# Soft mixture of experts behind a windowed attention: the order of the last unit, the selection of v, and two weight matrices in pieces

## The chip, the cores and the metric

One core of a Trainium2 chip runs the whole program. The metric is the device time of one execution in microseconds; the runs shown for the kernel before are three (184.94, 185.99 and 186.16 us, median 185.99). The profile is of one execution of its own.

The engines of the core are PE (matrix products, with its weight loads shown apart as PEld), DVE (elementwise work and reductions), ACT (activations and copies), POOL (here only an issuer of loads) and SP (issuer of stores). Sixteen DMA engines move data between main memory and the on-chip memory. PE writes to PSUM only.

## The reference

Eight batches, eight heads, 576 positions, 64 wide. Heads 0 to 3 attend to the last 32 positions, heads 4 to 7 to the last 128 positions in steps of 4 (the dilated heads). The outputs of the heads side by side are x, 4608 rows of 512. Then a soft mixture of experts:

```python
scores = np.where(masks, (1 / np.sqrt(D)) * q @ k.T, -1e9)       # per batch and head
x = softmax(scores) @ v                                          # 4608 x 512
logits = x @ phi                                                 # 32 slots, 4 for each of 8 experts
d = exp(logits - logits.max(0)); d /= d.sum(0)                   # over all tokens
slot_input = d.T @ x
for e in range(8): slot_out[e] = np.maximum(slot_input[e] @ w1[e], 0) @ w2[e]
c = exp(logits - logits.max(1)); c /= c.sum(1)                   # over the slots
return c @ slot_out
```

w1[e] is 512 x 1024, w2[e] is 1024 x 512. The slot inputs need the logits of every token, so no expert can start before the attention of the last batch is done, and no output before the last expert is.

## The kernel before

**Units.** The attention is cut into 32 units of two heads (NU = 4 per batch, in the order 0, 2, 1, 3 of `unit`, so that plain and dilated pairs alternate). A unit goes through `transposes` (q and k, L261), `scores` (L300), `softmax_parts` (Exp on ACT, then a product with the mask on DVE, L325), `values` (L367), a reciprocal and a product on DVE that make rows of x (L399, L400), and `x_transposes` (L409), which writes xT. The loop of L611 runs these for different units in one round, so that the engines overlap. In rounds of four, batch by batch, come `front_logits` (L432), `front_rows` (L462) and `front_slots` (L482), which add a batch to the slot inputs in `U_sb`. The last batch is done apart in `last_early`, `last_logits` and `last_slots` (L503 to L549), and ends in `siT` (L654), the slot inputs, transposed.

**Dilated keys and the last 64 positions.** A dilated head is worked on in four classes of positions (position mod 4), 144 positions to a class. 128 of a class make a full block (`P1`). The last 16 of each class stand in `P2` (L360), a block of 32 columns for each head, class and side (one side for keys among the first 128 of the class, one for the last 16), and `values` multiplies each with 32 columns of the array (L390 to L393).

**v.** The plain heads need v by blocks of 128 positions, and the load gives four positions to a partition. `select_v` (L198), once per batch, makes the blocks on PE: products of the raw v with `pick`, a 0/1 matrix, 32 partitions at a time at four places of the array. The last 64 positions come from a load of 16 partitions (`vt`). The results go through PSUM tiles `sel` (two from the pool ps_s, one from `ring`) and are copied by ACT to `vp` (L213, L234). `spread_v` copies the dilated v.

**PSUM.** ps_s has two buffers of two banks for the scores (and `sel`, and `last` in the end), ps_o two for the outputs of `values`, `ring` two for everything else: transposes, logits, rows, slots.

**Order.** A planner sets the order of PE, DVE and ACT from the order of the program, its costs and the free buffers. POOL's order is as written (L599).

**Loads.** POOL issues them all, with a cast from fp32 to fp16. Eight tiles `home` take the raw q, k and v of the eight batches (L154), all issued at the start. When batch e has been read out of its home, `load_w1(e)` and `load_w2(e)` (L236, L245) put the weights of expert e into it: 128 partitions, 1 MB of fp16 each, one transfer, w2[7] in two halves by columns. The order at the end is w1[6], w1[7], w2[6], w2[7]. Eight semaphores are used by turns for POOL's loads.

**Experts.** For each pair of experts `expert_in` (L670) makes the hidden values (64 matmuls L675 in all), ACT applies Relu (`hs`, L683), four transposes (L686) and two copies on DVE (`hTp`, L691) turn them, and `expert_out` (L696) adds to `sop` (L699, 8 matmuls per expert). The order is in(0), in(1), out(0), out(1), in(2), and so on. Then `so` is copied (L716), and for each of 36 blocks of 128 tokens a matmul (L735) and a scaling on ACT or DVE (L739, L741) make the output, stored by SP in 12 transfers (L745, L747).

## Time and profile before

| what | us |
|---|---|
| three runs: lowest, median, highest | 184.94, 185.99, 186.16 |
| profiled execution, from the first to the last instruction (span) | 183.5 |
| median of the runs less the span | 2.4 |
| PE busy, share of the span | 151.8, 83% |
| DVE | 117.1, 64% |
| ACT | 115.5, 63% |
| POOL | 46.9, 26% |
| last rows of x of the attention (L400) end at | 136.2 |
| first matmul of the experts (L675) starts at | 145.0 |
| last half of w2[7] has landed at | 156.74 |
| `so` copied at | 157.8 |
| first store issued at | 158.9 |

The page gives no own time for the profiled execution beside its span; what lies around the span is the start before the first instruction and the end after the last, and the table shows it only as the difference to the median of other runs. A row of the profile names the line, the engine, the operation and the tiles, then how often, how long in all, and in brackets how long the engine had been idle and what ended that. "L205 PE MATMUL sel<-home,pick" is a matmul of line 205 that writes a tile `sel` from `home` and `pick`; a group of rows close in time is merged, and its time then runs from the first start to the last end. A matmul's time includes its way through the array, so matmuls in a row overlap. PEclk is the granted clock of PE. The strips have 40 slices of the span.

### The profile page before, as it was taken

Reading aid. Unit: us, or ns where it says so; the run is one execution under the profiler, and the core shown is the slowest. Engines: PE = TensorE matmul, PEld = TensorE weight load, DVE = VectorE, ACT = ScalarE, POOL = GpSimd, SP = SyncE. Lnnn points to the kernel's source line nnn. Section 1 sums busy time; section 2 is a strip of 40 time slices with the busy share of each in tenths; the row PEclk is TensorE's granted clock in tenths of the full one; section 3 lists DMA queues with packets and bytes.
Section 4 is the critical chain, followed back from the end, with each engine's and each line's share of the span. In section 5 each row is a group of like instructions: output and inputs, shape, how many; then the busy total and the mean of one; then the engine's idle time right before and its main releaser. Section 6 shows DMA issues by size and latency. Waiting matters only on the chain.

```text
span 183.5 us, 6054 instructions
## 1 busy us (share of the span) xinstructions
PE 151.8 (83%) x2595; PEld 105.8 (58%) x2595; DVE 117.1 (64%) x363; ACT 115.5 (63%) x208; POOL 46.9 (26%) x77
## 2 busy tenths in 40 slices
PE   1869999999988989998997998898979998885300
PEld 1637776677676667666765767666768644432000
DVE  7605886388877877878779687786970111496410
ACT  2248845689599789779878959977703022675410
POOL 7752555464554654401102001003100000000000
PEclk9999999999999999999999999999995589998555
DMA  5999999999999999999999999999999995199996
GB/s 103 183 203 203 202 203 201 202 202 204 204 201 201 204 199 204 226 211 221 212 216 216 212 216 216 218 212 218 218 214 220 212 208 105 75 440 427 427 427 262
DMA packets 23978, 41.06 MB, mean 224 GB/s; under 512 B 1680, under 2 KB 20240, under 8 KB 21136
## 3 DMA queue, kind: packets, MB, share of 16 engines
q0 software_dynamic: 21584, 30.79, 93.9%
q1 hardware_dynamic: 2368, 9.89, 13.4%
q8 instruction: 20, 0.33, 0.6%
q14 instruction: 6, 0.05, 0.1%
HBM read 62.02 MB, written 9.44 MB: 389 GB/s over the span
## 4 chain that ended last, share of the span: by engine, by line
DMA 74%; issue 15%; POOL 3%; ACT 2%; DVE 1%; PE 0%; POOLq 0%; DVEq 0%; SPq 0%
DMA home<-in_moe_w_dram 31%; DMA home<-in_v_dram 15%; DMA home<-in_k_dram 12%; DMA home<-in_q_dram 9%; DMA out_dram<-ot 7%; ACT ot L739 2%; DVE ot L741 1%; POOL home L250 1%; POOL home L162 1%; POOL home L239 1%; POOL home L184 0%; POOL home L187 0%; ACT so L716 0%; PE sop L699 0%; PE f L735 0%
## 5 line engine op out<-in xcount | busy, mean ns | idle before, releaser
L400 DVE TENSOR_TENSOR x<-o,rc 128x384 f16<-128x384 f32 x64 | 29.9, 482 | 0.5
L332 ACT ACTIVATE pr<-s 128x960 f16<-128x960 f32 (+1 forms) x32 | 24.7, 780 | 1.8 <-PE s L315 1.8
L344 ACT ACTIVATE pd<-s 128x640 f16<-128x640 f32 x32 | 20.9, 706 | 1.7 <-PE s L315 1.7
L162 POOL DMA_DIRECT2D home<-in_v_dram x24 | 16.6, 692 | 16.6 <-DMA home<-in_k_dram 11.6
L205 PE MATMUL sel<-home,pick 32*128 32x256 f16 x128 | 17.8, 307 | 1.4 <-DMA home<-in_v_dram 1.1
L399 DVE RECIPROCAL rc<-o 128x6 f32<-128x6 f32 x64 | 10.2, 177 | 13.5 <-PE o L395 13.4
L416 PE MATMUL rgx<-ident,x 128*128 128x128 f16 x160 | 15.6, 233 | 3.0 <-ACT qT L295 3.0
L741 DVE TENSOR_SCALAR ot<-f,rrow 128x512 f32<-128x512 f32 (+1 forms) x19 | 12.5, 716 | 7.7 <-DMA out_dram<-ot 5.2
L335 DVE TENSOR_TENSOR Pp<-pr,mask 128x960 f16<-128x960 f16 (+2 forms) x48 | 16.4, 394 | 0.4 <-ACT pr L332 0.4
L280 ACT COPY qT<-rgq 128x576 f16<-128x576 f16 x16 | 10.3, 641 | 9.0 <-PE rgq L275 8.5
L422 ACT COPY xT<-rgx 128x512 f16<-128x512 f16 x16 | 9.6, 601 | 10.0 <-PE rgx L416 10.0
L739 ACT ACTIVATE ot<-f,rrow 128x512 f32<-128x512 f32 (+1 forms) x19 | 11.2, 675 | 7.0 <-DMA out_dram<-ot 6.6
L239 POOL DMA_DIRECT2D home<-in_moe_w_dram x8 | 4.3, 534 | 44.4 <-PE rgq L290 36.5
L213 ACT CAST vp<-sel 128x512 f16<-128x512 f32 x16 | 9.4, 590 | 9.2 <-PE sel L205 9.0
L416 PEld LDWEIGHTS <-x 128*128 128x128 f16 x160 | 10.2, 102 | 7.2 <-issue 5.4
L735 PE MATMUL f<-so,ET 128*128 128x512 f16 (+1 forms) x38 | 11.0, 402 | 3.9 <-ACT ot L739 3.0
L275 PEld LDWEIGHTS <-home 96*64 96x64 f16 x384 | 11.9, 123 | 3.9 <-issue 2.0
L184 POOL DMA_DIRECT2D home<-in_k_dram x16 | 10.6, 661 | 10.1 <-DMA home<-in_q_dram 8.2
L395 PE MATMUL o<-vp,Pp 128*128 128x65 f16 x288 | 12.9, 203 | 0.0
L436 PE MATMUL l<-xT,phi 128*128 128x288 f16 x64 | 10.8, 304 | 2.0 <-ACT qT L280 1.7
L295 DVE COPY kTd<-rgk 128x576 f16<-128x576 f16 x16 | 12.0, 752 | 0.6 <-PE rgk L290 0.5
L295 ACT COPY qT<-rgq 128x576 f16<-128x576 f16 x16 | 10.3, 646 | 3.1 <-PE rgq L290 2.6
(105 smaller groups left out, 292.9 us busy)
## 6 DMA issues: line engine op xcount, KB each, us to landing
home<-in_moe_w_dram POOLq DMA_DIRECT2D x15, 1024.0 KB, 30.1
out_dram<-ot SPq DMA_DIRECT2D x7, 1024.0 KB, 7.5
home<-in_k_dram POOLq DMA_DIRECT2D x16, 288.0 KB, 9.9
home<-in_q_dram POOLq DMA_DIRECT2D x15, 288.0 KB, 9.7
home<-in_v_dram POOLq DMA_DIRECT2D x16, 256.0 KB, 9.8
out_dram<-ot SPq DMA_DIRECT2D x3, 512.0 KB, 6.5
home<-in_moe_w_dram POOLq DMA_DIRECT2D x2, 512.0 KB, 27.3
home<-in_v_dram POOLq DMA_DIRECT2D x8, 64.0 KB, 8.9
```

The lines of the kernel that those rows point to most:

```text
L162: nc.gpsimd.dma_start(out=dst, in_=v[b, h0 : h0 + n_h, r0 : r0 + 4 * n_p, :].rearrange("h (p r) d -> p h (r d)", r=4),)
L205: nc.tensor.matmul(sel[:, n, 0], pick[rows, r].rearrange("p i j -> p (i j)"), raw[rows, :, r, :], start=(r == 0), stop=(r == 3), tile_posi ...
L275: nc.tensor.transpose(rg[64 * h : 64 * h + 64, r, :], raw[:, 2 * hp + h, D * r : D * r + D], ident[0:NP, 0:NP],)
L295: (nc.scalar.copy if nm == "q" else nc.vector.tensor_copy)(out=dst[:, 0:S].rearrange("c (g p a) -> c g p a", g=4, a=3), in_=rg.rearrange(" ...
L332: nc.scalar.activation(out=pr, in_=st[:, :, 0:n], func=AF.Exp, scale=SCALE)
L335: nc.vector.tensor_tensor(out=Pp[:, :, b0 : b0 + nb, 0:w], in0=pr[:, :, at : at + nb * w].rearrange("p h (t c) -> p h t c", c=w), in1=mask ...
L344: nc.scalar.activation(out=pr[:, part].rearrange("p c e t -> p e c t"), in_=st[:, :, 0 : 2 * DW].rearrange("p e (c t) -> p e c t", c=2), f ...
L395: nc.tensor.matmul(to, lhs, rhs, start=(n == 0), stop=(n == len(mms) - 1), skip_group_check=True)
L400: nc.vector.tensor_tensor(out=x[:, blocks[0] : blocks[0] + nb, D * hl : D * hl + 2 * D].rearrange("p t (h d) -> p t h d", h=2), in0=ot[:, ...
L416: nc.tensor.transpose(rg[:, 128 * blk : 128 * blk + 128], x[:, blk, hl : hl + 128], ident)
L739: nc.scalar.activation(out=ot[:, j, d0:d1], in_=fp, func=AF.Copy, scale=scale)
L741: nc.vector.tensor_scalar(out=ot[:, j, d0:d1], in0=fp, scalar1=scale, scalar2=None, op0=ALU.mult)
```

## The change

- **Selection of v.** `pick` has 128 partitions and 132 columns with one 1 in each row, so that a shifted window of 128 columns selects the wanted positions of all partitions: 16 matmuls of 128 rows in place of 16 of 32 rows. The end is 4 matmuls of 16 rows over all eight heads in place of 4 and 4. All three results are tiles of `ring`.
- **The last 16 of each class.** `P2` becomes `Pm` (keys among the first 128) and `Pt` (keys among the last 16), both as blocks of 128 columns with zeros between, made by two DVE products. `values` has five full matmuls per head for them in place of eight narrow ones. The rows of a class end are now in position order, so `x_transposes` copies them plainly, and the logits by rows have 9 blocks in place of 13.
- **Written order.** From the last unit on, PE, DVE and ACT run in the order of the program up to the end of the experts. The loop ends one round earlier, and what is left is written out. `fill` issues matmuls whose result nobody reads: two, one and two of 512 columns. The last logits by tokens go to ps_o. In the experts, `expert_in` of the next pair stands ahead of the transposes (`expert_turn`) and of `expert_out` of this pair.
- **Two w2.** w2[3] and w2[5] are loaded as 112 partitions, and then the last 16 partitions as four transfers of 8: one column block of eight, seven column blocks, one, seven.
- The constants change accordingly: `spread_masks` is gone, `spread_ends` is new, and the transposed phi is made by 16 matmuls in place of 4.

```diff
 RP, NP = 6, 96
 RD, ND = 12, 48
 CL = S // DIL
+TAIL = 16
 DW = CL + 16
 OUT_TILES = [(0, 2), (256, 2)] + [(512 + 512 * i, 4) for i in range(7)] + [(4096, 2), (4352, 2)]
 OUT_COLS = [sum(nj for _, nj in OUT_TILES[:i]) for i in range(len(OUT_TILES))]
 NU = 4 * B
 NV = 2
+UNEVEN = (3, 5)
 
...
-    pick = kept([128, 4, 32, 4], "pick")
+    pick = kept([128, 4, 132], "pick")
+    pick_end = kept([128, 4 * 144], "pick_end")
...
     def select_v(b):
         raw, last = raws[b]["vp"], raws[b]["vt"]
         for i in range(2):
-            sel = ps_s.tile([128, 2, 2, 4, D], FP32, name=f"sel{b}_{i}", tag="s")
-            for r in range(4):
-                for n in range(2):
-                    rows = slice(64 * i + 32 * n, 64 * i + 32 * n + 32)
+            sel = ring.tile([128, 2, 4, D], FP32, name=f"sel{b}_{i}", tag="ring")
+            for n in range(2):
+                for r in range(4):
                     nc.tensor.matmul(
-                        sel[:, n, 0],
-                        pick[rows, r].rearrange("p i j -> p (i j)"),
-                        raw[rows, :, r, :],
+                        sel[:, n],
+                        pick[:, 2 * i + n, 3 - r : 131 - r],
+                        raw[:, :, r, :],
                         start=(r == 0),
                         stop=(r == 3),
-                        tile_position=(64 * i + 32 * n, 0),
                     )
-            nc.scalar.copy(out=vp[b % NV][:, 2 * i : 2 * i + 2, :, 0:D], in_=sel[:, :, 0])
-        end = ring.tile([128, 2, 4, D], FP32, name=f"sel{b}_2", tag="ring")
+            nc.scalar.copy(out=vp[b % NV][:, 2 * i : 2 * i + 2, :, 0:D], in_=sel)
+        end = ring.tile([128, 2, 4, D], FP32, name=f"end{b}", tag="ring")
         for r in range(4):
             nc.tensor.matmul(
-                end[:, 0],
-                pick[96:112, r].rearrange("p i j -> p (i j)"),
-                last[:, 0:4, r, :],
+                end.rearrange("p a h d -> p (a h) d"),
+                pick_end[96:112, 128 * r : 128 * r + 128],
+                last[:, :, r, :],
                 start=(r == 0),
                 stop=(r == 3),
                 tile_position=(96, 0),
-            )
-        for r in range(4):
-            nc.tensor.matmul(
-                end[32 * r : 32 * r + 32, 1],
-                ident[96:112, 96:128],
-                last[:, 4:8, r, :],
-                start=True,
-                stop=True,
-                tile_position=(96, 32 * r),
-                skip_group_check=True,
             )
         nc.scalar.copy(out=vp[b % NV][:, 4:6, :, 0:D], in_=end)
...
     def load_w2(e):
         w2t = w_tiles[e][1]
         w2_from = moe_w2[e].rearrange("(p c) f -> p c f", p=128)
-        parts = ((0, 8),) if e < E_EXP - 1 else ((0, 4), (4, 8))
-        for c0, c1 in parts:
+        parts = [(0, 128, 0, 8)] if e < E_EXP - 1 else [(0, 128, 0, 4), (0, 128, 4, 8)]
+        if e in UNEVEN:
+            parts = [(0, 112, 0, 8)]
+            for p0 in (112, 120):
+                parts += [(p0, p0 + 8, 0, 1), (p0, p0 + 8, 1, 8)]
+        for p0, p1, c0, c1 in parts:
             nc.gpsimd.dma_start(
-                out=w2t[:, c0:c1].rearrange("p c f -> p (c f)"),
-                in_=w2_from[:, c0:c1].rearrange("p c f -> p (c f)"),
+                out=w2t[p0:p1, c0:c1].rearrange("p c f -> p (c f)"),
+                in_=w2_from[p0:p1, c0:c1].rearrange("p c f -> p (c f)"),
             )
 
...
+        tails = pr[:, :, :, 128:DW].rearrange("p a c (s t) -> p a c s t", s=2)
         nc.vector.tensor_tensor(
-            out=P2.rearrange("p a c s t -> p (a c) s t")[:, :, :, 0:16],
-            in0=pr[:, :, :, 128:DW].rearrange("p a c (s t) -> p (a c) s t", s=2),
-            in1=mask[:, QW + 64 :].rearrange("p (c s t) -> p c s t", c=8, s=2),
+            out=Pm.rearrange("p a (c x) -> p (a c) x", c=4)[:, :, 0 : 4 * TAIL : 4],
+            in0=tails[:, :, :, 0].rearrange("p a c t -> p (a c) t"),
+            in1=mask[:, None, 128:CL].broadcast_to([128, 8, TAIL]),
+            op=ALU.mult,
+        )
+        nc.vector.tensor_tensor(
+            out=Pt[:, :, 0 : 4 * TAIL].rearrange("p a (t c) -> p a c t", c=4),
+            in0=tails[:, :, :, 1],
+            in1=ends[:, None].broadcast_to([128, 2, 4, TAIL]),
             op=ALU.mult,
         )
...
                         mms.append((ot[:, i, h], P1[:, h, blk, :], vd[b % 2][:, 4 * (hl + h) + blk, :]))
                     else:
-                        for s in range(2):
-                            for c in range(4):
-                                vt = vp[b % NV][:, 5, hl + h] if s else vd[b % 2][:, 4 * (hl + h) + c]
-                                mms.append((ot[32 * c : 32 * c + 32, i, h], P2[:, h, c, s], vt))
+                        for c in range(4):
+                            mms.append((ot[:, i, h], Pm[:, h, 128 * c : 128 * c + 128], vd[b % 2][:, 4 * (hl + h) + c]))
+                        mms.append((ot[:, i, h], Pt[:, h], vp[b % NV][:, 5, hl + h]))
             for n, (to, lhs, rhs) in enumerate(mms):
                 nc.tensor.matmul(
...
+    def logits(b, c, lp, kcs):
+        for kc in kcs:
+            nc.tensor.matmul(
...
+    def token_weights(b, c, lp):
+        nc.scalar.activation(
+            out=ET[:, b * S + 288 * c : b * S + 288 * c + 288],
...
-    row_blocks = [(slice(0, 128), 128 * i, 1) for i in range(4)]
-    row_blocks += [(slice(0, 128), c, 4) for c in range(4)] + [(slice(0, 128), 512, 1)]
-    row_blocks += [(slice(32 * c, 32 * c + 32), 512 + c, 4) for c in range(4)]
+            logits(b, c, lp, range(4))
+            token_weights(b, c, lp)
+
+    row_blocks = [(128 * i, 1) for i in range(4)] + [(c, 4) for c in range(4)] + [(512, 1)]
 
     def rows(to, tokens, rhs, start, stop):
-        for n, (part, at, step) in enumerate(row_blocks):
-            w = step * (part.stop - part.start - 1) + 1
+        for n, (at, step) in enumerate(row_blocks):
             nc.tensor.matmul(
-                to[part, min(n, 9), :], tokens(at, at + w, step), rhs, start=start, stop=stop,
+                to[:, n, :], tokens(at, at + 127 * step + 1, step), rhs, start=start, stop=stop,
                 skip_group_check=True,
...
-    def last_early(last):
+    def last_open(last):
+        lr = last[:, 1, 0 : 10 * N_SLOTS].rearrange("p (i s) -> p i s", s=N_SLOTS)
+        nc.tensor.matmul(lr[:, 8], ident, shut, start=True, stop=False, skip_group_check=True)
+        return lr
+
+    def last_sums(last, lr):
         six = small.tile([128, 1], FP32, name="six")
         nc.vector.reduce_sum(six, csum, axis=AX.X)
         sixes = small.tile([128, N_SLOTS], FP32, name="sixes")
         nc.vector.tensor_scalar(out=sixes, in0=stackI, scalar1=six, scalar2=None, op0=ALU.mult)
+        nc.tensor.matmul(lr[:, 9], quarters, sixes, start=False, stop=False, skip_group_check=True)
...
     def last_slots(last, lr):
         er = Er[(B - 1) % 2]
-        nc.scalar.activation(out=er, in_=lr[:, 0:10], func=AF.Exp)
         for n, i in enumerate((0, 1, 2, 3, 8)):
...
-            )
+                lr[:, 9], ones, er[:, i, :], start=False, stop=(n == 4), skip_group_check=True
+            )
+        rtot = small.tile([128, N_SLOTS], FP32, name="rtot")
+        nc.vector.reciprocal(out=rtot, in_=lr[:, 9])
...
+        return rtot
...
+    def fill(to, n):
+        for _ in range(n):
+            nc.tensor.matmul(
+                to, ident, ET[:, 0:512], start=True, stop=True, skip_group_check=True
+            )
+
...
-        for r in range(4):
-            nc.vector.tensor_copy(out=pick[:, r, :, r], in_=stackI)
...
+        for t in range(4):
+            part = slice(32 * t, 32 * t + 32)
+            nc.vector.tensor_copy(out=pick[part, t, 3:128:4], in_=stackI[part])
+
+    def spread_ends():
+        for x, at, step in ((129, 0, 4), (144, 64, 1)):
+            nc.vector.tensor_copy(
+                out=pick_end[96:112, 0 : 4 * x].rearrange("p (r x) -> p r x", x=x)[
+                    :, :, at : at + 15 * step + 1 : step
+                ],
+                in_=ident[96:112, None, 96:112].broadcast_to([TAIL, 4, TAIL]),
+            )
...
-    for u in range(NU + 5):
-        if u + 1 < NU:
-            st = scores(u + 1)
-        if u < NU:
-            values(u)
-        if u + 1 < NU:
-            softmax_parts(u + 1, st)
+    for u in range(NU - 1):
+        st = scores(u + 1)
+        values(u)
+        softmax_parts(u + 1, st)
         if u + 3 < NU:
...
         b, ph = divmod(u - 4, 4)
-        if 0 <= b < B:
+        if b >= 0:
             if ph == 1:
-                if b == B - 1:
-                    last_logits(lr, 3)
-                    last_slots(last, lr)
...
-            elif ph == 3 and b < B - 1:
+            elif ph == 3:
                 front_slots(b)
         if u == 1:
             spread_phi()
-        if u == NU:
-            last = ps_s.tile([128, 2, 512], FP32, name="last", tag="s")
-            lr = last_early(last)
-        if 0 <= u - 1 < NU:
+        if u >= 1:
...
-    rtot = small.tile([128, N_SLOTS], FP32, name="rtot")
-    nc.vector.reciprocal(out=rtot, in_=lr[:, 10])
+    tail = tc.manual_schedule(
+        engines={mybir.EngineType.PE, mybir.EngineType.DVE, mybir.EngineType.Activation}
+    )
+    tail.__enter__()
+    last = ps_s.tile([128, 2, 512], FP32, name="last", tag="s")
+    lr = last_open(last)
+    last_logits(lr, 0)
+    last_logits(lr, 2)
+    values(NU - 1)
+    x_transposes(NU - 2)
+    front_slots(B - 2)
+    spare = ps_s.tile([128, 2, 512], FP32, name="spare", tag="s")
+    last_logits(lr, 1)
+    fill(spare[:, 0], 2)
+    x_transposes(NU - 1)
+    last_sums(last, lr)
+    lps = [ps_o.tile([128, 288], FP32, name=f"l{B - 1}_{c}", tag="o") for c in range(2)]
+    for c in range(2):
+        logits(B - 1, c, lps[c], range(3))
+    last_logits(lr, 3)
+    er = Er[(B - 1) % 2]
+    nc.scalar.activation(out=er, in_=lr[:, 0:9], func=AF.Exp)
+    for c in range(2):
+        logits(B - 1, c, lps[c], (3,))
+        token_weights(B - 1, c, lps[c])
+    fill(spare[:, 0], 1)
+    rtot = last_slots(last, lr)
...
     )
+    fill(spare[:, 1], 2)
+    front_rows(B - 1)
...
-        hs = small.tile([128, 512], FP16, name=f"hs{pr}", tag="hs")
+        hs = hss[pr] = small.tile([128, 512], FP16, name=f"hs{pr}", tag="hs")
         nc.scalar.activation(out=hs, in_=hp_, func=AF.Relu)
+
+    def expert_turn(pr):
+        hs = hss[pr]
...
+    expert_in(0)
     for pr in range(4):
-        expert_in(pr)
-        if pr >= 1:
-            expert_out(2 * pr - 2)
-            expert_out(2 * pr - 1)
-    expert_out(6)
-    expert_out(7)
+        if pr < 3:
+            expert_in(pr + 1)
+        expert_turn(pr)
+        expert_out(2 * pr)
+        expert_out(2 * pr + 1)
+    tail.__exit__(None, None, None)
```

## The prediction

> **What bounds the kernel now.** I read the page's strip of 40 slices first, then its queue table, the chain that ended last, the table by stage over the last microseconds of loading, and last the instructions in order of time.
>
> The strip (slices of 4.59 us) and the queue table:
> ```profile
> PEclk9999999999999999999999999999995589998555
> DMA  5999999999999999999999999999999995199996
> ...
> q0 software_dynamic: 21584, 30.79, 93.9%
> ...
> q8 instruction: 20, 0.33, 0.6%
> ```
> The DMA engines are full from the first slice to the 33rd, run out in the next two and are full again while the output is written. The only software queue, POOL's loads, is busy 93.9%. The chain agrees:
> ```profile
> 128.48 28.27 DMA home<-in_moe_w_dram
> 156.74 0.04 issue
> 156.78 0.42 PE sop L699 x4
> ```
> The last half of w2[7] was issued at 128.0 and landed at 156.74, behind a queue 28 us long. After it come only four matmuls (L699), the copy of `so` (L716, 0.59 us) and the output (12 transfers, DMA bound at about 2.45 us per MB). So the time is: when the last w2 lands, or when the experts are ready if that is later, plus a tail that the change leaves alone.
>
> The stages just before, with the DMA share in the last column but one:
> ```profile
> 152.00:153.00 1.00, 0.69 (x12) 0.38 (x12) 0.07 (x1) 0.42 (x1) 0.00 (x0) 1.00 0.66 131
> 153.00:154.00 1.00, 1.00 (x24) 0.57 (x20) 0.18 (x2) 0.00 (x0) 0.00 (x0) 1.00 0.55 111
> 154.00:155.00 1.00, 0.81 (x16) 0.22 (x8) 0.00 (x0) 0.53 (x1) 0.00 (x0) 1.00 0.47 98
> 155.00:156.00 1.00, 0.87 (x15) 0.57 (x19) 0.26 (x2) 0.07 (x1) 0.00 (x0) 1.00 0.14 29
> 156.00:157.00 1.00, 0.94 (x19) 0.41 (x11) 0.00 (x0) 0.00 (x0) 0.00 (x0) 1.00 0.02 4
> ```
> The engines do not finish together. At 153.5 about 0.55 x 16 = 9 work, at 154.5 between seven and eight, at 155.5 about two. The shares from 152 on add up to 1.84 us of all 16, so in perfect balance the load would end near 153.9, 2.8 us sooner: no division of the same bytes can gain more. The trace's sixteen landing marks per load say whose lateness it is: all engines take 4.87 us per matrix, but after each of the 20 packets of 16 KB in q8 (0.94 us each) one engine is about 1.1 us later for good, and the hit goes round **eight** engines. By the end seven engines lie within 1.0 us of the first (152.2), nine are 2.0 to 4.5 us behind, the last two hit three times. I take them for blocks of PE's program: 0.33 MB over its 2 x 2595 instructions would be 63 B for one.
>
> The compute is nearly as late. The last x rows (L400) end at 136.22, the first expert matmul (L675) starts at 145.03, and the experts run to 157.2 with 0.44 us of that spent on the last load. Without it `sop` would end at 156.75.
>
> **The change, part by part.**
>
> *The two w2 in pieces.* Each engine now moves 8 rows of such a matrix. After, 112 rows give every engine 7, and 16 rows come as four transfers of 8 rows: 1 KB, 7 KB, 1 KB, 7 KB of fp16 per row. The packets of q0 took 60 ns at 512 B, 135 at 1536, 324 at 4096, 625 at 8192, and 22 for the 4 B of a completion: about 0.10 us for 1 KB and 0.55 for 7 KB. Full rows follow each other at 0.60, so 0.02 of each overlaps: 0.08 and 0.53, and at most 0.06 for four more completions. No transfer of the trace has 8 rows; such a one can feed at most eight engines. If both large ones go to one half of the engines and both small ones to the other, a matrix gives the one half -0.60 + 0.16 + 0.06 = -0.38 us and the other -0.60 + 1.06 + 0.06 = +0.52. Two matrices: **-0.76 and +1.04**. If all four fall on one half, that one gets +1.2 and the other -1.1. If they scatter, a late engine can gain or lose the same. Which half is PE's no row shows. I take -0.76 for the late eight, at two to one, which is a choice and no reading: the early seven then end by 154.2, the ninth late one at 155.3, the rest at 155.98. So `sop` ends at 156.4 in place of 157.2.
>
> The Trainium skill ("DMA: Bandwidth & Descriptors", section "Why a DMA increments its semaphore by 16 and not by 1") says that a SWDGE transfer of 8 partitions runs on 8 consecutive engines from a round-robin cursor. By that both large pieces of each matrix fall on the same eight, so the sum is one of two, -0.76 or +1.04, and not a scatter; no run here shows it. The same page (section "Anatomy of one DMA") fits about 2.0 us fixed per DMA, which would make eight more transfers cost 16 us; the trace speaks against it for queued loads: the two halves of w2[7] land 2.46 and 2.47 us apart (mean over the engines), where a whole matrix takes 4.87 to 4.93, so one more costs 0.06 us at most.
>
> PE loses some 155 matmuls of 2595 (6 per dilated unit, 4 per batch in select_v and 4 in the rows, 16 at the end, less 17 new ones), so about one of the 20 blocks; the last engine's third hit, at 130, only moves. Nothing.
>
> *POOL and its window.* Eight more issues at 0.53 us are 4 us on a queue that is 26% busy. But POOL also waits for old loads:
> ```profile
> 83.06 0.53 POOL L239 DMA_DIRECT2D home<-in_moe_w_dram  x1 [5.40 <-DMA home<-in_moe_w_dram]
> ...
> 126.91 0.53 POOL L239 DMA_DIRECT2D home<-in_moe_w_dram  x1 [14.42 <-PE rgq L290]
> ```
> w1[4] was issued when w1[0], eight loads before, had landed (82.53): eight in flight. Five pieces fill five of eight places, so w1[4] waits for w1[2] (102.0), w1[6] for w1[4] (121.5), w1[7] for w2[4] (126.4, as now), w2[6] for w1[5] (132.5). At each of these at least three matrices, 15 us, are still queued. Cost nothing; without that cover every microsecond of dry queue is one of time.
>
> *selection of v.* Before, per batch: 16 matmuls of 32 rows (four in 0.39 us, one in 0.28: 0.04 each), 4 of 16 rows (four in 0.59: 0.10 each), 4 to separate columns (almost free): 1.0 us of PE. After: 16 of 256 columns at the unpaired 0.10 and 4 of 512 at 0.19: 2.3 us, **+1.3**. Against it, the two `sel` tiles leave ps_s, where today they hold back the next scores:
> ```profile
> 121.73 0.39 PE L205 MATMUL sel<-home,pick 32*128 32x256 f16 x4
> ...
> 122.16 0.59 ACT L213 CAST vp<-sel 128x512 f16<-128x512 f32 x1 [0.18 <-PE sel L205]
> ...
> 124.81 0.59 ACT L213 CAST vp<-sel 128x512 f16<-128x512 f32 x1 [0.96 <-PE sel L205]
> ...
> 125.37 0.51 PE L315 MATMUL s<-qT,kTd 64*128 64x144 f16 x16
> ```
> Of the 14.95 us of that batch ACT is idle 2.5, some 2.0 of it around these copies. They now compete for `ring`'s two buffers with the transposes.
>
> *The dilated ends.* P2 (L360, 0.28 us on DVE) becomes Pm and Pt of 128 elements each; the nearest form (L335, 128x128) takes 0.22, so +0.16 us per dilated unit, 0.3 per batch; values has 10 matmuls for 16 narrow ones, 0.1 us either way. DVE is idle 2.3 us per batch, which covers it.
>
> Together a batch can be 1.6 us longer (all of it on the path) or 2.0 shorter (all that idle time gone): +11 to -14 us over seven batches. I take 0, as the three engines are each busy about 12.5 to 13 of 15 us and one gains what another loses.
>
> *The written tail.* In the order written, DVE finishes x of the last unit before the U_sb sum (0.66 us, now between them): x ends 0.5 us sooner. PE then waits for xT of unit 30 (0.45), does 9 row matmuls (0.3) and two fills (0.43), the last five transposes (0.45), waits for `sixes` behind DVE's copy (0.7), ten fp32 matmuls (2.3, at the rate of L509), six logits (0.72), nine rows (0.5). Exp 0.44, 45 small matmuls 1.5, siT and hand-over 0.5: 8.3 us, where 8.8 stand now. First expert matmul at 144.0. The experts take one `expert_in` (0.9), transposes (0.41), copies and hand-over (0.46), 16 out (0.87): 2.64 us per pair, as the pairs take now at full clock; ready at 154.6. The strip shows half clock where PE thins out, and by the stages it ran from 138.0 to 148.2; if that comes again in spite of the fills, this part is about 1.8 us longer: 156.4.
>
> Sum: last load 156.74 - 0.76, `sop` at 156.4, compute 154.6 to 156.4 beside it. **-0.76 us** on the profiled execution, span 183.5 to 182.8. The runs' median lies 2.4 us above the span (lowest 1.4); that I leave as it is: **185.2 us**.
>
> **Rivals.**
>
> *The other half.* Large pieces on the engines that PE's blocks delay: last load 157.8, +1.0 us, **187.0**. For it: nothing in the trace names the engines. Against: nothing either. 0.24.
>
> *A longer attention.* The new matmuls and the two ring buffers put more on the path than ps_s gives back. The compute then decides, once x is later than now by 1.8 us at full clock or at once at half clock. With half of the +11 it is ready at 160 to 162: +3 to +5, **189 to 191**; beyond +4.5 at full clock (2.7 at half) it is over 1%. Until about 9 us w1[7] still reaches a queue that is not dry. For it: PE is busy 18 of 20 us in those stages. Against: that counts each matmul to its modelled end, the weight loads fill only 13.6 of 20, and ACT's idle time lies in just this part. 0.20.
>
> *All four pieces on the early half.* -1.1 us, **184.9**; 0.04. *A cost per transfer.* At the 0.06 of the row above, eight more take 0.5 us on every engine and leave -0.3; that lies inside the forecast. (By the page's 2.0 us it would be some 202; the row leaves that no chance worth a number.) *No effect*, the pieces spread evenly and the compute still beside them: +0.1, **186.1**; 0.06. The forecast keeps 0.46.
>
> **How the numbers follow.** The forecast, even with the runs' lowest in place of their median, gives 184.2. The range reaches 184.0 below and 188.6 above: it holds the other half and the mild part of the longer attention, and leaves its worse part out, about 0.12. One per cent (1.86 us) is about what a measurement of this kernel can tell from no change. Faster by more: only if attention and loads both gain more than worked out, 0.05. Slower by more: nearly all of the longer attention plus the other half with a compute that is late as well, 0.22. Within: 0.73.
>
> **What would show it.** Right: the share of DMA engines busy falls later and more steeply, the last w2 lands near 156.0 and the chain still goes through it and four L699. Wrong in the pieces: landing near 157.8. Wrong in the attention: L699 waits for `hTp` and not for a load, and the last L400 ends after 138. Wrong in the tail: half clock through the experts. A dry queue would show as an idle DMA slice before the 33rd.

## The result, and the profile after

The changed kernel takes **199.84 us** (median of four runs, 198.92 to 204.65), the kernel before 185.76 beside it: a ratio of 1.074, with an interval of 1.069 to 1.079. It is 14 us slower. The forecast was 185.2 us, its range 184.0 to 188.6. Some executions of most kernels here are disturbed, some per cent longer, and count in the medians but not in the ratios: the profile below is of one (span 202.9 us), so I read its stages and not its end, and after_one_piece and ends_first_copies, below, have too few others for a ratio.

The strip (slices of 5.07 us), the queue table and a part of the chain that ended last, of the changed kernel:
```profile
PEclk9999999999999969999999999999995559999555
DMA  5999999999999999999999999993499600079997
...
q0 software_dynamic: 21808, 30.79, 85.6%
```
```profile
139.79 1.85 PE sel L212 x16
141.64 0.98 PE end L222 x4
...
142.65 0.60 ACT vp L230
...
175.06 1.08 PE sop L719 x16
```
The DMA engines, full up to the 33rd slice before, run out in the 28th, and for three slices before the output they do nothing. The chain no longer goes through a load: the last w2 lands at 161.8, `sop` is ready at 176.1. In each batch the chain goes through the selection, then ACT's copy of it.

Where the time goes, per batch. The windows of two batches, from the first `rc` of one batch to that of the second next, of the kernel before and of the changed one (columns: window, its length, busy us of PE, PE's weight loads, DVE, ACT, POOL, then the clock, the DMA share and GB/s):
```profile
81.39:111.37 29.98, 27.31 (x580) 20.31 (x577) 23.95 (x72) 24.76 (x47) 2.12 (x4) 1.00 1.03 216
```
```profile
77.01:110.04 33.03, 30.16 (x539) 22.95 (x536) 24.81 (x76) 25.13 (x47) 4.21 (x8) 1.00 1.03 215
```
A batch grew from 14.99 to 16.52 us at full clock, and PE's busy time by 1.43 of it. That reads as if the longer matmuls of the selection were the cause. The experiments say that by themselves they are not.

### The profile page after: what moved, and what is told of

It reads as the page before. It is cut to its first block, busy times and chain, and to the rows that moved or that the text cites. A ratio compares the mean times of both kernels' runs of the same rounds, so it can differ in the third digit from the quotient of the medians.

```text
span 202.9 us, 5736 instructions
## 1 busy us (share of the span) xinstructions
PE 165.4 (82%) x2440; PEld 115.9 (57%) x2440; DVE 121.4 (60%) x375; ACT 116.3 (57%) x208; POOL 51.2 (25%) x85
## 3 DMA queue, kind: packets, MB, share of 16 engines
q1 hardware_dynamic: 2368, 9.89, 12.3%
## 4 chain that ended last, share of the span: by engine, by line
PE 34%; DMA 33%; DVE 17%; ACT 7%; issue 3%; POOL 2%; DVEq 0%; SPq 0%; ACTq 0%; POOLq 0%
DMA home<-in_v_dram 13%; DMA home<-in_k_dram 9%; DMA out_dram<-ot 6%; DMA home<-in_q_dram 5%; PE sel L212 5%; PE l L436 5%; DVE x L406 4%; PE rgx L422 3%; PE s L315 3%; DVE kTd L295 3%; PE o L401 3%; PE end L222 2%; PE h L692 2%; PE sop L719 2%; ACT xT L429 2%
## 5 line engine op out<-in xcount | busy, mean ns | idle before, releaser
L332 ACT ACTIVATE pr<-s 128x960 f16<-128x960 f32 (+1 forms) x32 | 23.2, 761 | 2.4 <-PE s L315 2.4
L344 ACT ACTIVATE pd<-s 128x640 f16<-128x640 f32 x32 | 22.7, 717 | 1.8 <-PE s L315 1.6
L405 DVE RECIPROCAL rc<-o 128x6 f32<-128x6 f32 x64 | 11.5, 182 | 18.4 <-PE o L401 18.2
L335 DVE TENSOR_TENSOR Pp<-pr,mask 128x960 f16<-128x960 f16 (+2 forms) x48 | 17.6, 385 | 5.3 <-ACT pr L332 5.3
L212 PE MATMUL sel<-home,pick 128*128 128x256 f16 x128 | 18.9, 310 | 0.1
L422 PE MATMUL rgx<-ident,x 128*128 128x128 f16 x160 | 15.6, 233 | 4.0 <-ACT qT L295 2.5
L422 PEld LDWEIGHTS <-x 128*128 128x128 f16 x160 | 11.9, 103 | 7.4 <-issue 6.4
L212 PEld LDWEIGHTS <-pick 128*128 128x128 f16 x128 | 13.5, 111 | 4.1 <-issue 0.8
L315 PE MATMUL s<-qT,kTd 64*128 64x144 f16 (+1 forms) x256 | 15.8, 209 | 0.0
L250 POOL DMA_DIRECT2D home<-in_moe_w_dram x17 | 8.8, 525 | 26.8 <-DMA home<-in_moe_w_dram 16.4
L426 DVE COPY xT<-rgx 128x576 f16<-128x576 f16 x16 | 7.3, 453 | 12.9 <-PE rgx L422 12.9
L756 PE MATMUL f<-so,ET 128*128 128x512 f16 (+1 forms) x38 | 11.1, 404 | 4.0 <-ACT ot L760 3.1
L235 POOL DMA_DIRECT2D home<-in_moe_w_dram x8 | 4.4, 545 | 37.8 <-PE rgq L290 23.4
```

Source lines behind the costliest of these rows:

```text
L212: nc.tensor.matmul(sel[:, n], pick[:, 2 * i + n, 3 - r : 131 - r], raw[:, :, r, :], start=(r == 0), stop=(r == 3),)
L315: nc.tensor.matmul(st[:, g, at : at + n], kT[64 * g : 64 * g + 64, ks : ks + 128], qT[64 * g : 64 * g + 64, q0 : q0 + n], start=True, stop ...
L332: nc.scalar.activation(out=pr, in_=st[:, :, 0:n], func=AF.Exp, scale=SCALE)
L335: nc.vector.tensor_tensor(out=Pp[:, :, b0 : b0 + nb, 0:w], in0=pr[:, :, at : at + nb * w].rearrange("p h (t c) -> p h t c", c=w), in1=mask ...
L344: nc.scalar.activation(out=pr[:, part].rearrange("p c e t -> p e c t"), in_=st[:, :, 0 : 2 * DW].rearrange("p e (c t) -> p e c t", c=2), f ...
L422: nc.tensor.transpose(rg[:, 128 * blk : 128 * blk + 128], x[:, blk, hl : hl + 128], ident)
```

## The experiments

Theory A at first: PE's time in the selection lies on the path. Theory B: the dilated ends with their two products on DVE and the swapped copies. "Batch" in this table is the mean of four, from the first `rc` of unit 12 to that of unit 28 in the kernel's profile; the four of select_alone, ring_quarter, dve_dose, ends_alone, ends_first_copies, after_old_select, tail_alone and pieces_cursor_2 hold stretches of half clock (0.50 in PEclk), so a batch of theirs at full clock is shorter.

| kernel | median us | ratio to before, interval | batch us |
|---|---|---|---|
| before (profile of the prediction) | 185.99 | | 14.95 |
| changed | 199.84 | 1.074, 1.069 to 1.079 | 16.51 |
| pieces_alone | 186.6 | 1.003, 0.9995 to 1.006 | 14.93 |
| select_alone | 199.4 | 1.059, 1.053 to 1.065 | 17.93 |
| ends_alone | 188.4 | 1.011, 1.007 to 1.016 | 15.49 |
| tail_alone | 185.5 | 0.999, 0.996 to 1.002 | 15.26 |
| select_in_ps_s | 185.99 | 1.001, 0.998 to 1.004 | 14.95 |
| copies_swapped | 185.64 | 0.997, 0.992 to 1.002 | 14.88 |
| after_old_select | 190.32 | 1.023, 1.016 to 1.030 | 15.62 |
| after_one_piece | 202.74 | none | 16.52 |
| ring_quarter | 200.67 | 1.068, 1.063 to 1.073 | 17.94 |
| after_ps_s | 187.53 | 1.007, 1.004 to 1.011 | 15.36 |
| ends_first_copies | 191.27 | none | 15.55 |
| dve_dose | 194.97 | 1.047, 1.042 to 1.053 | 16.70 |
| end_in_ps_s | 185.95 | 1.001, 0.998 to 1.004 | 15.00 |
| pieces_cursor_2 | 186.49 | 1.003, 1.000 to 1.007 | 15.72 |
| pieces_cursor_14 | 186.31 | 1.003, 0.999 to 1.006 | 14.92 |
| two_undone | 187.21 | 1.007, 1.003 to 1.010 | 15.08 |
| ps_s_old_tail | 185.54 | 0.999, 0.996 to 1.003 | 15.36 |
| ps_s_one_piece | 187.17 | 1.003, 0.998 to 1.007 | 15.35 |

### Each part alone

Each of these puts one part of the change on the kernel before, with that part's lines of the diff: `load_w2` with UNEVEN; the 16 matmuls and `sel` in `ring` (the old `end` kept); P2 to Pm and Pt with the nine row blocks, the four-matmul `end` and the copy order that go with them; the written tail with the order of the experts.

> The kernel before with the two w2 in pieces and nothing else. My forecast: the two large pieces fall on one half of the engines, the last load lands 0.76 us sooner (or 1.04 later if it is the other half), and with the attention as before the time moves by -0.8 or +1.0 us. A rival, a fixed cost of about 2 us per transfer: eight more transfers, +16 us, which would be the whole loss of the changed kernel. A second rival, the window of eight loads in flight runs dry: the last load lands several us later with idle DMA engines before it.

> The kernel before with the selection of v over all 128 rows into tiles of ring (and the phi products that use the same matrix), its ends as before. Theory A, the loss is PE's time in the selection, on the path: in the changed kernel's trace the 16 matmuls take 1.85 us in one block, once per batch at full clock and 3.8 at half clock in the first batch; here about +1.0 us per batch and +3 in the beginning, some +9 to +11 us, period of a batch 16 us in place of 14.9. Theory B, the loss is the dilated ends (two DVE products of 0.45 and 0.50 us in place of one of 0.28) and the swapped copies: here no more than +1 us.

> The kernel before with the new dilated ends alone (Pm and Pt, full blocks of 128 columns, 9 row blocks, the copy of the last 64 columns ahead of the copy of the first 512, the v ends of all heads in one group of matmuls); selection of 32 rows, end of the program and loads as before. Theory A (selection): within 2 us of before. Theory B (ends and copies): +0.67 us on DVE per dilated unit, 1.3 per batch, and ACT's copy behind DVE's: +8 to +11 us, period of a batch about 16.3 us.

> The kernel before with the written order from the last unit on and the fills, nothing else. The forecast had 8.3 us from the last x to the first expert matmul where 8.8 stand; the changed kernel's trace shows 11.1 at half clock. If that comes from the written order, here too about 11, and the experts 1.0 us shorter: the experts ready some 1 to 1.5 us later than now, time +1 to +1.5 us. If it came only from the later loads and the disturbed clock, the time stays within 0.5 us, since the last load decides.

By the ratios the selection alone brings +11 us, the ends +2.1, the tail and the pieces nothing that can be told. As far as the sums go, theory A holds; the next runs took it apart.

### Not the matmuls but where their result stands

select_in_ps_s has the same 16 matmuls over all rows; only the tile differs from select_alone:
```diff
-            sel = ring.tile([128, 2, 4, D], FP32, name=f"sel{b}_{i}", tag="ring")
+            sel = ps_s.tile([128, 2, 2, 4, D], FP32, name=f"sel{b}_{i}", tag="s")
```


> The kernel before with the 16 matmuls of the selection over all 128 rows, as in select_alone, but with the two `sel` tiles left in ps_s, where they stand in the kernel before; the 4 + 4 matmuls of `end` as before. Theory A (PE's time): the 16 matmuls take 1.9 us in place of 0.7 per batch wherever their result stands, nothing hides it, and this kernel is as slow as select_alone, 195 to 199 us; the block of 8 shows 0.93 to 0.95 us at full clock. Theory R (the ring): the `sel` tiles in `ring` hold back the transposes and x; with the tiles back in ps_s most of the +11 us goes, 186 to 190 us, though PE still does the longer matmuls.

185.99 us: **all of the loss is gone** with the long matmuls in place. Theory A falls, theory R holds. The converse, ring_quarter, keeps the tiles in `ring` and takes the matmuls away, one in four left, so vp holds only a quarter of what is chosen:
```diff
-                for r in range(4):
+                for r in range(1):   # start=True, stop=True
```


> The kernel select_alone (selection over all rows, `sel` in `ring`) with three of every four matmuls of the selection left out: r = 0 alone, 4 matmuls per batch in place of 16, so vp holds only a quarter of the chosen rows. PE's time in the selection is then about 0.5 us per batch, below the 0.7 us of the kernel before. Theory P (place: the two tiles in `ring` by themselves hold the transposes and x back, whatever the matmuls cost): most of the +11 us stays, 192 us or more, and the batch stays above 16 us. Theory M (a block of PE in a bad place: the loss is the 1.9 us of matmuls that PE does in one stretch at a point where DVE and ACT have nothing else): the loss goes with the matmuls, 186 to 188 us, batch 15.0 to 15.3.

200.67 us, a loss at least as large as select_alone's, so taking matmuls away does not bring the time back. But part of this loss is the clock's. The one batch of ring_quarter that ran wholly at full clock, and one that did not (columns as above):
```profile
34.08:49.87 15.79, 13.54 (x284) 10.19 (x281) 12.04 (x38) 13.18 (x26) 8.75 (x13) 1.00 1.31 203
...
86.77:106.29 19.52, 18.02 (x280) 13.00 (x278) 11.83 (x37) 12.69 (x24) 1.06 (x2) 0.67 1.03 216
```
At full clock it is 15.79 us, against 16.61 to 16.67 in select_alone and 14.85 to 15.13 in the kernel before. So at full clock the place costs 0.7 to 0.9 us per batch even with a quarter of the matmuls, and the other three quarters, in that place, some 0.8 more; the other batches of ring_quarter, 17.0 to 19.5 us, hold 4.3 to 12.7 us of half clock each. The amount of matmul does matter, but only where the result stands in `ring`. The same edit as in select_in_ps_s, made on the changed kernel:

> The changed kernel with one edit: the two `sel` tiles of the selection over all rows stand in ps_s, as in select_in_ps_s, and not in `ring`. If the place of `sel` is the whole loss of the selection also here, this is as fast as after_old_select, 189 to 191 us, in spite of the 16 long matmuls, with a batch of about 15.6 us as there. If the long matmuls cost something behind the dilated ends (less idle time on PE than alone), 192 to 195.

187.53 us: the pool that `sel` is taken from is 12.3 of the 14 us.

Why, in order of time. The changed kernel around one selection (start, length, engine, line, operation, what, how often; in brackets the engine's idle time before and what ended it):
```profile
105.92 0.44 PE L422 MATMUL rgx<-ident,x 128*128 128x128 f16 x5
105.98 0.68 DVE L507 TENSOR_TENSOR U_sb<-U_sb,u 128x512 f32<-128x512 f32 x1
...
106.72 1.91 PE L212 MATMUL sel<-home,pick 128*128 128x256 f16 x16
...
107.79 0.59 ACT L219 CAST vp<-sel 128x512 f16<-128x512 f32 x1
108.56 1.03 PE L222 MATMUL end<-home,pick_end 16*128 16x512 f16 x4
...
109.53 0.60 PE L401 MATMUL o<-vp,Pp 128*128 128x65 f16 x14
109.63 0.59 ACT L230 CAST vp<-end 128x512 f16<-128x512 f32 x1 [0.38 <-PE end L222]
...
109.96 0.29 PE L290 MATMUL rgq<-ident,home 96*128 96x96 f16 x3
110.04 0.20 DVE L405 RECIPROCAL rc<-o 128x6 f32<-128x6 f32 x1 [1.76 <-PE o L401]
...
110.52 0.42 PE L290 MATMUL rgk<-ident,home 96*128 96x96 f16 x6
```
`ring` has two buffers, given out in the order of the program: `up` (`u` in the rows), `rgx`, then the two `sel`, `end`, then `rgq` and `rgk` of the next unit. So the first `sel` waits until `up` has been added into U_sb (ends 106.66, `sel` starts 106.72), `end` until ACT has copied the first `sel` (ends 108.38; PE is busy with the second `sel` until about then, too), `rgk` until ACT has copied `end` (ends 110.22, `rgk` starts 110.52). The selection cannot begin earlier, and what comes after it cannot pass it. The first `o` of the new batch needs vp and stands behind it too, and DVE waits 1.76 us.

The same place in select_in_ps_s:
```profile
103.72 0.50 PE L203 MATMUL sel<-home,pick 128*128 128x256 f16 x3
...
104.06 0.44 PE L413 MATMUL rgx<-ident,x 128*128 128x128 f16 x5
...
104.34 0.27 PE L203 MATMUL sel<-home,pick 128*128 128x256 f16 x1
...
106.94 0.69 DVE L498 TENSOR_TENSOR U_sb<-U_sb,u 128x512 f32<-128x512 f32 x1 [0.17 <-PE u L486]
...
107.31 0.60 PE L203 MATMUL sel<-home,pick 128*128 128x256 f16 x4
...
109.04 0.72 PE L392 MATMUL o<-vp,Pp 128*128 128x65 f16 x18
...
109.60 0.42 PE L287 MATMUL rgq<-ident,home 96*128 96x96 f16 x6
```
In ps_s the selection begins 3.2 us ahead of the U_sb sum, and its matmuls go in ones to fours into gaps between the transposes, the sums and the slots of the batch. Its PE time is then free: a batch takes 14.95 us as in the kernel before, and in two batches PE is busy 27.56 us against 27.31 (matmuls that overlap count once).
```profile
79.66:109.56 29.90, 27.56 (x580) 21.01 (x577) 23.94 (x73) 24.93 (x47) 2.12 (x4) 1.00 1.03 215
```
One measure holds all of them together, the stretch from the end of the U_sb sum to the next unit's first `rgq`: 1.79 us in the kernel before (in all six batches), 1.96 to 1.97 in select_in_ps_s, 1.88 to 2.32 in after_ps_s, 3.30 to 3.33 in the changed kernel at full clock, 3.77 to 3.78 in select_alone and 3.11 in ring_quarter where each ran at full clock, 4.3 to 6.7 where they ran at half. The changed kernel's +1.5 us in it is the batch's +1.5. In ring_quarter, with a quarter of the selection's matmuls, it is still +1.3: the tiles and their copies stand in a row.

The parts of the 12.3, as an estimate: seven batches at 16.51 - 15.36 = 1.15, all taken at full clock, give 8.1. The first `rc` comes at 21.1 in after_one_piece against 18.2 in after_ps_s, 2.9 more (20.8 to 23.2 in the four kernels with both `sel` in `ring`, 20.0 at most in all others). That makes 11.0; 1.3 I can't allot, and the early batches at half clock differ by more than that from one profile to the next.

Is it each tile that costs? In the kernel before one tile of the selection, `end`, stands in `ring`. Taken out:
```diff
-        end = ring.tile([128, 2, 4, D], FP32, name=f"sel{b}_2", tag="ring")
+        end = ps_s.tile([128, 2, 2, 4, D], FP32, name=f"sel{b}_2", tag="s")
```


> The kernel before with one edit: the `end` tile of the selection, the one that stands in `ring` there, is put into ps_s, so that no tile of the selection stands in `ring`. If each tile of the selection in `ring` costs time by itself (three there cost some 1.6 us per batch against one), the batch shrinks from 14.95 to 14.2 to 14.7 us; the time stays at 185 to 186 us, since the last load decides. If one tile in `ring` costs nothing, or ps_s is now the one that is held: batch 14.9 to 15.3.

No gain: a batch of 15.00. One tile there costs nothing, three with all their matmuls cost 1.2 to 1.8. With two buffers, one tile leaves the other to go round, which would agree; two tiles were not tried.

### The rest of the change, undone by parts

> The changed kernel with one part undone: the selection of v and of phi on 32 rows with `sel` in ps_s, as in the kernel before. Theory A (selection is nearly all of the loss, and what is left is the dilated ends): 187.5 to 189.5 us, compute and load nearly together at the end. If the parts only add up as run alone (+0.8 pieces, +2.1 ends, -0.3 tail), 188.4. Theory T (the written tail costs more behind a late x than alone): above 190.

> The changed kernel with every w2 loaded in whole rows, as in the kernel before; all else as changed. In the changed kernel the compute decides the end, by 14 us over the last load. So 199 to 200.5 us, the same as the changed kernel's 199.84. If the five pieces filling POOL's window of eight matter after all (a load issued late and a queue run dry that holds the experts), 196 to 198.

after_old_select (190.32 us) stays above both the sum of the parts and after_ps_s. DVE's first microseconds show most of why, after_old_select first, then after_ps_s:
```profile
14.53 1.09 DVE L590 CAST phi_by<-phi_sb 32x128 f16<-32x128 f32 x4
...
16.41 0.69 DVE L298 COPY kTd<-rgk 128x576 f16<-128x576 f16 x1
...
19.98 0.20 DVE L408 RECIPROCAL rc<-o 128x6 f32<-128x6 f32 x1 [1.81 <-PE o L404]
```
```profile
14.64 0.69 DVE L295 COPY kTd<-rgk 128x576 f16<-128x576 f16 x1
...
18.21 0.20 DVE L405 RECIPROCAL rc<-o 128x6 f32<-128x6 f32 x1 [1.94 <-PE o L401]
```
The old selection comes with an old form of phi, cast in four parts. In the three kernels that join it to the new dilated ends (ends_alone, ends_first_copies, after_old_select) these casts stand at 14.2 to 15.6 us, among DVE's first work for the units; in all other kernels the casts of phi are over by 9.3, while DVE waits for loads. The first `rc` then comes 1.8 us later, and that is 1.8 of the 3.0 us by which the last batch begins later than in after_ps_s. In ends_alone, too, 1.5 of the +2.1 us stand at the first `rc` already (19.75 against 18.23). So the order on DVE, and not the selection's matmuls, seems to do it; no run moved the casts alone. after_one_piece tells only that the pieces do not carry the loss.

On after_ps_s, 1.5 us over the kernel before, I then undid one part at a time: the ends, the tail, the pieces.

> The changed kernel with two things undone: `sel` in ps_s in place of `ring`, and the dilated ends (32-row tiles, one product P2) as in the kernel before; what stays is the selection over all rows, the pieces, the written tail and the swapped copies. If the place of `sel` and DVE's two products are the whole loss: 185 to 186 us, no slower than before, batch 14.9 to 15.0, and after_ps_s's 187.53 minus this (some 2 us) is the price of the dilated ends. If something else of the change costs, 186.5 to 188.

> after_ps_s (the changed kernel with `sel` in ps_s) with the loop's end, the last unit and the experts in the order of the kernel before. If the written tail carries the 1.5 us that after_ps_s still lies above the kernel before: 185.5 to 186.3 us. If the tail is neutral here, as in tail_alone: 187 to 188.

> after_ps_s with w2[3] and w2[5] in whole rows. Its last load should land at 156.7 in place of 157.32. If the pieces carry the rest of after_ps_s's loss: 186 to 186.8 us. If not (the compute is the later one there as well): 187 to 187.8.

Without the dilated ends the batch is shorter (15.08) but the time the same, 187.21. Both end on the compute, so seven batches shorter by 0.28 us should show; why they don't I can't tell (batch 0 of two_undone's profile, mostly at half clock, took 19.0 us). With the old tail the time falls to **185.54 us**, at the kernel before, with ends and pieces in place. The two intervals to the kernel before, 0.996 to 1.003 and 1.004 to 1.011, do not meet. So the rest is the **written tail**, which alone had cost nothing. Without the pieces, 187.17: not to be told from after_ps_s. ps_s_old_tail ends on the load again, after_ps_s on the compute (the chains of both, in this order):
```profile
136.23 20.81 DMA home<-in_moe_w_dram
...
157.08 0.42 PE sop L695 x4
```
```profile
156.04 0.36 PE tp L706 x4
...
156.42 0.18 DVE hTp L711
...
156.65 1.14 PE sop L719 x16
```
No version beat the kernel before.

### DVE: products, copies, and a dose

copies_swapped moves DVE's copy of 64 columns ahead of ACT's copy of 512; ends_first_copies is ends_alone with ACT's copy first again; dve_dose makes the product for P2 three times, twice into an unused tile:
```diff
+        nc.vector.tensor_tensor(out=P2x..., in0=pr..., in1=mask..., op=ALU.mult)   # twice
         nc.vector.tensor_tensor(out=P2..., in0=pr..., in1=mask..., op=ALU.mult)
```


> The kernel before with one edit: for a dilated unit, DVE's copy of 64 columns of xT is written ahead of ACT's copy of 512 columns, and is contiguous columns as in the changed kernel only in place, not in form. Theory B1 (the swap holds ACT back behind DVE's copy, as in the profile of the changed kernel, where ACT waited 13 times, 14.1 us, for it): most of the +2.1 us of ends_alone is here, 187.5 to 188.5 us. Theory B2 (DVE's two products of 0.45 and 0.50 us where one of 0.28 stood): 185.5 to 186.2 us here, no change, and the +2.1 comes from the products.

> The kernel ends_alone (dilated ends as in the changed kernel) with ACT's copy of 512 columns of xT written ahead of DVE's copy of 64, as in the kernel before. Theory B1 (the order of the copies costs once the ends are there): 185.5 to 187 us and a batch of 15.0 to 15.2. Theory B2 (DVE's two products of 0.45 and 0.50 us in place of one of 0.28): 187.5 to 189 us, batch 15.6 as in ends_alone.

> The kernel before with the product for P2 (0.28 us on DVE) done three times per dilated unit, twice into a tile that nobody reads: +0.56 us of DVE per dilated unit, 1.1 per batch, and nothing else. Theory B2 (DVE's added time lies on the path of the batch whatever its idle share): the batch grows by 0.4 to 0.8 us from 14.95, and the time is 186.5 to 188.5 us. If DVE's 2.3 us of idle time per batch cover it, as the prediction had it: batch 14.9 to 15.1, 185.5 to 186.3 us, and the ends must cost in another way.

The copies cost nothing: 185.64 us alone, and with the ends the batch is 15.55 in the one order and 15.49 in the other. For the longer batch this leaves the two products and the ends' new matmuls, which no run took apart; that DVE's time can do it, the dose shows. The dose of 1.12 us of DVE per batch cost far more than I expected, 9 us. Two windows of dve_dose show why, a batch with a window of half clock and one of full:
```profile
102.41:105.82 3.41, 2.27 (x62) 1.89 (x63) 3.41 (x12) 2.82 (x6) 0.33 (x1) 1.00 1.02 214
105.82:109.24 3.42, 3.42 (x32) 2.25 (x31) 1.17 (x4) 2.26 (x7) 0.00 (x0) 0.50 1.02 216
```
DVE is busy for all of 3.41 us, PE waits for it and is busy 2.27 of them, and in the next 3.41 us PE has half its clock: the logits (L449, 8 matmuls) of that batch take 2.01 us, at full clock 1.21. The batch that ran at full clock throughout (first `rc` 118.13 to 133.80) takes 15.67, +0.72 for 1.12 us of DVE; those with the window take 17.04.

### The pieces, moved to other engines

```diff
+        if e == 2:
+            parts = [(0, 112, 0, 8), (112, 114, 0, 8)]   # cursor_14: 126
...
+        if e == 5:   # rows 114 (cursor_14: 126) to 127 of w2[2]
```


> The kernel pieces_alone with w2[2] in three transfers: rows 0 to 111 and 112 and 113 in its place, rows 114 to 127 only behind w2[5]; the pieces of w2[3] and w2[5] then should fall on engines two further on, and every engine still has 8 rows of w2[2]. The reading of pieces_alone: the small pieces meet six of the eight engines that PE's program delays and two of the others. If that is right, one of pieces_cursor_2 and pieces_cursor_14 meets eight of eight (all late ones relieved: last load 156.0, 185.2 us) and the other four (last load 157 to 157.8, 186.3 to 187 us). If the two land alike, within 0.3 us of pieces_alone's 156.86, the engines are not taken in such an order, and the reading falls.

> As pieces_cursor_2, but rows 112 to 125 of w2[2] go first and the last two rows behind w2[5]: fourteen engines further on, which is two back. Expected: the opposite of pieces_cursor_2; the better of the two at 185.2 us with the last load near 156.0, the worse at 186.3 to 187.

The last load lands at 156.86 us in pieces_alone, at 157.42 with the pieces two engines on, and at 156.13 fourteen on: up and down, as expected. But these are one profile each. The pieces of pieces_alone land between 156.31 and 157.32 in four other kernels (after_old_select, two_undone, ps_s_old_tail, after_ps_s), and 156.13 and 157.42 lie only 0.2 and 0.1 us outside that. So it is not shown that the engines of such transfers follow one another. In the Trainium skill ("DMA: Bandwidth & Descriptors", section "Why a DMA increments its semaphore by 16 and not by 1") a transfer on fewer than 16 engines takes consecutive ones from a cursor; 156.13 and 157.42 would fit that. The time did not follow: the median of pieces_cursor_14 is 186.31 against an expected 185.2, though the profiled execution itself took 185.32. In that profile PE had waited 1.26 us for the load, and from 157.6 to 161.0 it had half its clock, just where the first output tiles need it; there the kernel before had full clock. From the last load to the end of the span it is 27.3 us against 26.8 in the kernel before.

## Why the prediction was wrong

- **"They now compete for `ring`'s two buffers"**, in the selection's step, and its sum "I take 0": this is the step that failed. I saw the two tiles leave ps_s and counted that as a gain of up to 2.0 us of ACT's idle time per batch, set against PE's +1.3 us as the price, and put the wait for `ring` at nothing. No kernel in which the tiles leave ps_s shows a gain (changed 16.51, select_alone 16.67 at full clock). The price is the row of `ring`, +1.2 to +1.8 us per batch; PE's matmuls are free in ps_s (batch 14.95 with the old ones and the new) and make up some 0.8 us of that price in select_alone, where their tiles stand in the row.
- **The rival "a longer attention"** had the two buffers in it and was right in kind. Its size, half of +11 us, was not: seven batches at 16.51 against 14.95 are all of the 11, and the start came on top. The reason given against it did not bear on it: that PE's busy time counts to a modelled end says nothing for or against a tile that waits its turn.
- **"DVE is idle 2.3 us per batch, which covers it."** The products took 0.45 and 0.50 us, +0.67 per dilated unit where the prediction had +0.16 from the wrong form. The idle time covered only part: the ends make +0.28 per batch (15.36 in after_ps_s, 15.08 in two_undone), the dose +0.72. That the ends cost nothing in the time of ps_s_old_tail is the load's doing, which ends that kernel, not DVE's.
- **The written tail.** x of the last unit was to come 0.5 us sooner; from `rc` of unit 30 to that of unit 31 it is 4.36 us in after_ps_s, 2.73 in ps_s_old_tail. From x to the first expert matmul the forecast had 8.3 us; it took 12.4 in tail_alone and 11.1 in the changed kernel. The half clock began before the first fill (152.8 against 154.5 us in the changed kernel), and the five fills did not end it, as this window shows:
```profile
154.00:159.00 5.00, 4.14 (x27) 3.33 (x28) 1.27 (x5) 0.59 (x1) 0.00 (x0) 0.50 1.01 206
```
  Half clock "in spite of the fills" was foreseen at 1.8 us; in the changed kernel it began ahead of the last rows of x and lasted until 166.5. The experts were right: 2.56 us per pair, forecast 2.64.
- **The pieces** were to give -0.76 or +1.04. pieces_alone lands at 156.86, +0.12 on the kernel before, but kernels with the same loads differ by more: 156.31 to 157.32 in five with these pieces, 155.55 to 156.74 in nine without. By the medians of these (156.86 and 156.11) the pieces land later, if anything, and -0.76 was the wrong choice. I had taken it for one half of the engines or the other. That the small pieces met some of the late engines and some early ones may be; no record names an engine. Each transfer more cost nothing: the mean landing of the last load is 154.06 us against 154.15. The issue window cost nothing, as said. The dry queue came from elsewhere: w1[7] was issued at 143.5, since POOL waits for the units, which were late; this is the case that the prediction named with 9 us.
- **"The compute is nearly as late"** was a reading of one execution. Its first batches ran late at half clock; in copies_swapped, with the same time, the last unit comes 4.3 us sooner. This slack is what covers the ends' longer batch in ps_s_old_tail.

## What to carry to other kernels

Moving a tile from one pool to another moves its place in a queue: list the tiles of the new pool in the order of the program, and for each new one see what must be released before it can start and what waits behind it, before any matmul is counted. An engine's idle share says little of what one more instruction costs; add a dose of it and look. Where work is left out to test a cause, compare batches at the same clock, for PE with less to do may be given less clock. And a part that is neutral alone may cost in the final kernel, so undo parts there too.

## What the runs showed of the hardware

The clock of PE falls though PE is busy most of the time. In dve_dose stretches of 3.41 us with 2.17 to 2.29 us of busy PE were followed by 3.41 us at half clock, five times, one in each of five batches; in tail_alone 2.24 and 2.36 us were. In the kernel before, 2.40 and 2.46 us were not. The Trainium skill ("TensorE: Matmul & The Clock Gate", section "Part 1: The HAM clock gate (the "warmup" mystery)") gives the same window of about 3.4 us, but says that an idle one lowers the clock; here one that was busy two thirds did. Busy time is not the whole rule: in ring_quarter six stretches of 2.54 to 2.82 us were followed by half clock, and ahead of the tail of the kernel before, one of 2.88. With such a window in each of five batches dve_dose settled at 17.04 us per batch, which is five times 3.41.
